# Zero products in TensorE's idle time, half-width contractions and a new order in a GQA decode and gated MLP backward kernel

## The chip, the cores and the metric

The kernel runs on one core of one Trainium2 chip. Times are device microseconds of one execution, from the runs' own clock. A profile is one execution recorded by the hardware; its span goes from the first to the last instruction of the program.

## The reference

A layer of one token for two sequences: grouped-query attention over a cache (32 query heads, 16 key heads, 4096 positions, head size 128) beside a gated MLP without activation (576 to 4608 and back), both on a layer-normed input, summed with the input. The kernel must give the output and the gradients of every input, all in bf16.

```
xn  = layernorm(x)                       # x: 2 x 1 x 576
q   = xn @ wq                            # 32 heads of 128
p   = softmax(q @ k_cache.T / sqrt(128)) # two query heads share one key head
a   = (p @ v_cache) @ wo
h   = (xn @ w_gate) * (xn @ w_up)
out = x + a + h @ w_down
# returned: out, and the vector-Jacobian product with grad_out for
# x, k_cache, v_cache, wq, wo, w_gate, w_up, w_down
```

The caches are 2 x 16 x 4096 x 128 each, and so are their gradients. The gradient of the values is an outer product of p and the output gradient, that of the keys an outer product of ds and q. So 92 MB are read, 92 MB are written, and little is computed on each element.

## The kernel before

**Work.** The attention goes in 16 steps: a step is one pair of key heads (a "group" of two) of one sequence, and loads four tiles of 1 MB, two of K and two of V, each 128 partitions by 4096. `load_kv` issues these loads on SyncE (SP); `load_ws` issues those of the weights, `put` the stores, on the same queue, in order. For each step:

- `turn` transposes K and V tiles in 32 x 32 blocks on VectorE (DVE), two instructions of 1024 fp32 pairs per tile, into another buffer of the pool `big`.
- `score` (L1205) multiplies the transposed tile by small stationaries `W`, 32 products a tile; four products with 32 output partitions stand side by side on the array.
- `softmax` and `dscore` turn the scores into p and ds through a chain of small products and copies on ScalarE (ACT), DVE and TensorE (PE) (L1267 to L1333), and `spread` brings them into the two layouts `pp` and `dd`.
- `contract` (L1378) multiplies the K or V tile as it was loaded by `pp` or `dd`: 16 products of 512 columns a step for each of K and V, in halves of 8, four side by side in one PSUM bank. Its end, with the transposes, sets the tile free for the next load (`free_kv`). The bank is copied to `osb` (L422 or L1388), and four products with `fold` (L1395) sum it into `oT`.
- `outer` and `head_outer` (L1226) make the outer products, two of 512 columns for each 128 x 1024 piece, into the three double banks `o`; ACT or DVE copies each piece to a 1 MB buffer of `big` (L422, L424), which `put` stores (L644).
- GpSimd builds the block-diagonal `BD` (L1193) and the stationaries `W` (L1170).

The MLP comes in nine pieces (`mlp`) with outer products of the same kind, and the gradients of wq and wo are made once a group (`group_back`).

**PSUM.** Six of the eight banks are the three double banks `o`; the two banks `m` serve all the rest, one user at a time.

**Order.** Nothing is scheduled at run time. While the program is built, the class `Order` plays through all streams of work with a cost for each operation, and writes each engine's instructions in the order in which they would start. Ties within a small slack go by the priorities `PRI`; `AT` says at which load of K or V the weights are loaded; `EV` lets each eviction go to ACT or DVE, whichever would be done first, with `BIAS` against DVE. A product's cost is its streaming time times `CLK`. The engines then run their lists in order and wait on semaphores, whatever the costs were.

```
def PE(stream, issue=0.0, quad=None, kind="f"):
    return ("op", "PE", max(CLK * stream, issue) + 0.03, quad, stream, issue, kind)
```

The functions that the change touches:

Of the kernel before, what the change touches and what calls it, by code (L numbers as in the profile page):

```python
# [63 lines left out]
class Order:  # L64
# [88 lines left out]
    def run(self):  # L153
        while self.streams:
# [94 lines left out]
def DMA(engine, cost, nbytes, row=8192):  # L249
# [7 lines left out]
    "turn0": [12127.5, 6592.3, 21769.7, -2605.1, 16027.7, 11327.0, 15999.3, 39550.4, 10382.6, -7734.4, 35538.2,  # L257
        24878.1, 2718.9, 31584.2, -26890.5, 2784.8],
    "turn1": [-17638.3, 2610.3, 11642.0, -23025.1, -666.2, 15183.7, -8429.9, 1153.7, -20487.3, 25941.4,
        10117.7, 4947.3, -2272.2, 26485.5, 30929.5, -2450.0],  # L260
    "W0": [17499.7, 23187.9, 23229.4, -24562.1, -25413.4, 21241.8, -52583.1, 25355.3, -4026.7, -26992.9,
        -2792.0, -39509.0, -20712.1, -23397.7, -38581.5, -1973.1],
    "W1": [-68220.0, -3785.6, -5692.6, -26672.7, -32830.2, -16110.0, -12761.0, -19860.2, 22087.6, 15126.8,
        -21980.3, 8805.5, -32643.6, 50340.4, -9766.7, -46949.6],
    "BD0": [33847.1, 15885.5, -3782.4, -11229.3, 24201.3, 31507.4, 16705.2, 36715.7, 22613.4, -26234.1,
        -2581.7, 109848.8, -44765.9, -8040.0, -3442.2, 23039.7],
    "BD1": [6023.1, 63457.9, 25871.9, 3200.3, 32198.5, -18814.1, 12365.4, 26532.9, 45847.1, -51895.6, 27362.3,
        -76393.3, 2863.2, -15443.1, -42340.1, -14044.7],
    "att": [-30329.0, -12134.6, -9680.1, 2262.2, -4349.2, 5413.2, -20317.8, -14023.7, -15815.4, -22206.1,
        -49797.4, -334.9, -19593.2, -20211.8, -68161.8, -27358.0],  # L270
    "dsc": [-23906.4, -34630.7, -2728.5, -23998.0, -19328.5, -8575.3, -10061.5, -15550.8, 13655.4, -23902.2,
        -28324.1, -40880.7, -28538.6, -56867.0, -5830.5, -12006.5],
    "conv": [-12341.8, -11809.0, -28772.8, 4652.6, -75297.7, -7012.1, -20664.5, 17461.5, 27449.8, 21658.4,
        -6850.8, -13921.3, -10206.6, -13431.8, 19855.6, -8570.5],
    "con": [-42900.2, 17788.3, 198.2, -17106.1, -21976.4, -3999.9, 7207.3, -22623.4, -6927.6, 21516.2, 20924.0,
        -13390.2, -118243.2, -7700.5, 19019.7, 14780.5],
    "out0": [22678.2, 12788.2, 42398.2, 31027.3, 49279.4, -11087.6, 5917.5, 42793.0, -20399.7, 57105.8,
        29375.6, 687.4, 24906.2, -2550.4, -27276.1, 33869.5],
    "out1": [19262.8, 2604.4, 2928.7, 23228.2, 21627.8, -10501.4, 15188.8, 7961.4, 18967.4, 20607.5, 11898.0,
        33332.1, 33685.2, 22220.0, 30731.2, 4846.1],  # L280
    "load": [27975.6, -31596.9, -27237.7, 3512.0, -22563.4, -17007.1, 4137.9, 25122.5, 5758.3, -9052.6,
        -35105.2, 2003.7, -28928.7, 6812.9, 23298.4, -60102.7],
    "front": [22268.9, 9016.8, -3195.4, -925.0, -11488.9, -5594.5, -10266.7, 2816.4],
    "back": [8334.8, 3131.5, 10704.4, -20159.0, -16008.9, -4698.0, -5371.8, 1371.3],
    "mlp": [-5535.1, -15193.4, -221.7, -14784.7, -3773.2, 8812.5, 807.2, 180.8, 6936.3],
    "mload": [-52363.2, -31069.0, 25120.7, -76464.9, 11215.5],
    "wload": [26545.8, -25483.3, -28807.4, 17849.2, -51701.7, -14210.9, -857.7, -9350.9, -12979.9, -24368.0,
        -173571.7, -10429.5, -11015.2, 13337.1, -10805.0, 6634.5],
    "wout": [-3917.3],
    "store": [6257.1],  # L290
    "fin": [-45349.8],
    "const": [46567.9],
}
AT = {
    "wq": [-5, 7, 11, 24, 31, -18, 50, -5],
    "wo": [-13, -2, -15, 2, 36, -14, 47, 53],
    "mlp": [2, 16, -13, 39, 111],
# [13 lines left out]
def kernel(  # L311
# [81 lines left out]
    osb_t = tiles("osb", 1, [P, 4, P])  # L393
# [15 lines left out]
    m_t = banks("m", 2, [P, 512])  # L409
# [29 lines left out]

    eps_t = filled("eps_t", [2, 1], FP32, EPS)  # L440
# [38 lines left out]
    fold = const.tile([P, 4, GH], BF16, name="fold")  # L479
    foldf = ch_t[0]["ex"][:, 80:80 + 4 * GH].rearrange("p (w r) -> p w r", w=4)  # L480
# [6 lines left out]
    def consts():  # L487
# [18 lines left out]
        for w in range(4):  # L506
            sums(foldf[:, w].rearrange("p (l r) -> p l r", l=2), [[32, 2], [1, 2], [64, 2]], 4 * w)
# [746 lines left out]
    def softmax(s):  # L1254
# [6 lines left out]
        for l in range(G):  # L1261
            yield PE(0.427, 0.224, kind="c")
            score(0, s, sc, l)
            yield REL("X", xS[s][0][l])
        yield REL("W0", wS[s][0])
# [15 lines left out]
        nc.tensor.matmul(mT[:, 256:257], lhsT=c["mr"][:], rhs=one1[:], start=True, stop=True)  # L1281
        yield DVE(0.14)
        nc.vector.tensor_scalar(c["negb"][:], mT[:, 256:257], -SCALE, None, op0=ALU.mult)  # L1283
# [26 lines left out]
    def dscore(s):  # L1310
# [4 lines left out]
        for l in range(G):  # L1315
            yield PE(0.427, 0.224, kind="c")
            score(1, s, dp, l)
            yield REL("X", xS[s][1][l])
        yield REL("W1", wS[s][1])
# [41 lines left out]
    def contract(s, t):  # L1361
# [11 lines left out]
        for part in range(2):  # L1373
            yield PE(0.427, 0.056, kind="c")
            for k in range(8 * part, 8 * part + 8, 4):
                for j in range(4):
                    c, l = k + NCH // 2 * (j // 2), j % 2
                    nc.tensor.matmul(ct[32 * j:32 * j + 32, :], lhsT=view(rT, 0, P, 4 * c + 2 * l, [[1, 32]]),  # L1378
                                     rhs=kv_t[kvS[s][t][l]][:, Dh * c:Dh * (c + 4)],
                                     start=(k == 0), stop=(k == NCH // 2 - 4))  # L1380
# [3 lines left out]
        e = yield EV(512)  # L1384
# [8 lines left out]
        yield PE(0.0, 0.104)  # L1393
        for w in range(4):
            nc.tensor.matmul(m_t[m][:, 0:GH], lhsT=osb_t[i][:, w], rhs=fold[:, w], start=(w == 0), stop=(w == 3))  # L1395
# [138 lines left out]
```

## Time and profile before

| | |
|---|---|
| median of 3 runs | 472.77 us (471.36 to 472.91) |
| the profiled execution | 471.37 us |
| its span | 469.6 us |
| mean granted TensorE clock in it | 0.71 |
| HBM read, written | 92.48 MB, 92.48 MB |

A row of a group gives line, engine, operation, output and inputs, shape, count, then busy us, mean ns of one, and the idle time in front of them with what ended it. PEld is the weight load, which runs beside the products. A window's row gives start:end, length, busy us (and instructions) of PE, PEld, DVE, ACT and POOL, then the granted clock, the mean busy share of the 16 DMA engines, and GB/s. In the 40 slices of the page each digit is a tenth of the slice's time.

### The profile page before, as it was taken

The page shows a single profiled execution, that of the slowest core. Times are in us where ns is not written, and L with a number is a line of the kernel's source. Part 1 is how long each engine was busy: PE and PEld are TensorE (multiplying, and loading weights), DVE is VectorE, ACT ScalarE, POOL GpSimd, SP SyncE. Part 2 cuts the span into 40 slices and gives each one's busy share as a digit, 9 for nine tenths or more (in the row PEclk, how much of TensorE's full clock was granted, in tenths as well). Part 3 has the DMA queues.
Part 4 walks back from the last instruction along what each step waited for, and adds up shares of the span by engine and source line. Part 5 has one row for each costly group of instructions (what it writes and reads, how often), then busy time and mean ns, then how long its engine had stood idle before and what let it go on. Part 6 is the DMA issues. An engine that isn't in the chain of part 4 may idle for free.

```text
span 469.6 us, 15459 instructions
## 1 busy us (share of the span) xinstructions
PE 370.8 (79%) x6636; PEld 217.5 (46%) x6636; DVE 369.5 (79%) x705; ACT 334.3 (71%) x507; POOL 146.8 (31%) x176
## 2 busy tenths in 40 slices
PE   0588688869887777986997669789699898998984
PEld 0455444435653352554463444564345434444453
DVE  9689878967867879688689658978867978898772
ACT  2149668867885948671798638877678678789973
POOL 3350242681330320203252264000843705325100
PEclk9978897767757668776675767956656658566977
DMA  8999999999999999999999999999999989999995
GB/s 317 404 413 403 363 390 419 409 416 421 418 416 420 399 421 406 412 415 419 399 418 404 386 418 424 408 413 342 413 416 393 424 270 416 423 413 413 424 368 176
DMA packets 40053, 185.96 MB, mean 396 GB/s; under 512 B 3496, under 2 KB 11184, under 8 KB 23600
## 3 DMA queue, kind: packets, MB, share of 16 engines
q1 hardware_dynamic: 39976, 184.96, 98.1%
q8 instruction: 52, 0.85, 0.7%
q14 instruction: 17, 0.14, 0.1%
q10 hardware_dynamic: 8, 0.00, 0.0%
HBM read 92.48 MB, written 92.48 MB: 394 GB/s over the span
## 4 chain that ended last, share of the span: by engine, by line
PE 42%; ACT 18%; DVE 18%; DMA 12%; issue 5%; POOL 2%; SPq 2%; ACTq 0%; DVEq 0%; POOLq 0%
ACT big L422 15%; DMA out_dram<-big 10%; DVE big L418 8%; PE ps_m L1378 8%; PE ps_o L1226 7%; PE ps_m L1205 7%; PE ps_o L675 4%; PE ps_m L841 3%; DVE big L424 3%; DMA big<-in_A_v_cache_dram 3%; PE ps_m L967 2%; PE ps_m L636 2%; POOL BD L1193 2%; PE ps_o L712 1%; SPq L1129 1%
## 5 line engine op out<-in xcount | busy, mean ns | idle before, releaser
L422 ACT CAST big<-ps_o 128x1024 bf16<-128x1024 f32 (+4 forms) x319 | 279.7, 950 | 40.3 <-PE ps_o L1226 18.2
L418 DVE STREAM_TRANSPOSE big<-big 128x1024 f32<-128x1024 f32 x146 | 176.1, 1223 | 5.9 <-DMA big<-in_A_v_cache_dram 3.6
L1193 POOL TENSOR_TENSOR BD<-vr,mask 128x2048 bf16<-128x2048 bf16 x32 | 115.2, 3603 | 198.8 <-ACT vr L422 122.2
L424 DVE CAST big<-ps_o 128x1024 bf16<-128x1024 f32 (+2 forms) x71 | 78.2, 1102 | 15.8 <-PE ps_o L675 5.2
L1205 PE MATMUL ps_m<-big,W 128*32 128x128 bf16 x2048 | 57.1, 274 | 5.5 <-ACT osb L422 0.7
L1226 PE MATMUL ps_o<-BD,dd 32*128 32x512 bf16 x256 | 48.8, 489 | 12.7 <-ACT big L422 9.2
L1205 PEld LDWEIGHTS <-W 128*32 128x32 bf16 x2048 | 45.4, 121 | 21.9 <-issue 18.6
L1226 PE MATMUL ps_o<-BD,pp 32*128 32x512 bf16 x256 | 42.1, 461 | 10.4 <-ACT big L422 6.7
L1170 POOL COPY W<-rep 32x16 bf16<-32x16 bf16 x128 | 24.5, 192 | 63.5 <-DVE rep L951 53.2
L418 DVE STREAM_TRANSPOSE big<-ww 128x1152 f32<-128x1152 f32 (+1 forms) x25 | 32.9, 1317 | 4.5 <-DMA out_dram<-big 3.3
L1378 PE MATMUL ps_m<-big,pp 128*32 128x512 bf16 x256 | 28.2, 536 | 1.5 <-DVE small L1330 1.2
L1378 PE MATMUL ps_m<-big,dd 128*32 128x512 bf16 x256 | 27.5, 518 | 1.5 <-DVE dd L418 0.6
L1226 PEld LDWEIGHTS <-dd 32*128 32x128 bf16 x256 | 11.8, 97 | 32.4 <-issue 24.7
L1226 PEld LDWEIGHTS <-pp 32*128 32x128 bf16 x256 | 10.4, 95 | 26.9 <-issue 22.6
L422 ACT CAST osb<-ps_m 128x512 bf16<-128x512 f32 x15 | 8.9, 590 | 15.9 <-PE ps_m L1378 12.6
L675 PE MATMUL ps_o<-dyr,R 32*32 32x288 bf16 x256 | 17.3, 402 | 2.0 <-ACT big L422 2.0
L675 PE MATMUL ps_o<-dyr,hb 32*32 32x288 bf16 x288 | 16.5, 346 | 1.1 <-ACT big L422 0.9
L967 PE MATMUL ps_m<-big,Wdy 128*128 128x128 bf16 x144 | 14.9, 285 | 3.1 <-DVE small L1283 2.0
L712 PEld LDWEIGHTS <-xnr 32*128 32x128 bf16 x368 | 12.5, 119 | 9.3 <-issue 8.6
L422 ACT CAST sp<-ps_m 128x256 bf16<-128x256 f32 x22 | 8.4, 380 | 11.2 <-PE ps_m L1213 11.0
L636 PEld LDWEIGHTS <-wm 128*32 128x32 bf16 x704 | 13.4, 115 | 6.3 <-issue 5.1
L841 PE MATMUL ps_m<-big,Wdy 128*128 128x128 bf16 x162 | 15.6, 272 | 0.6 <-DVE small L1291 0.4
(210 smaller groups left out, 481.9 us busy)
## 6 DMA issues: line engine op xcount, KB each, us to landing
out_dram<-big SPq DMA_DIRECT2D x74, 1024.0 KB, 12.1
big<-in_A_k_cache_dram SPq DMA_DIRECT2D x32, 1024.0 KB, 12.4
big<-in_A_v_cache_dram SPq DMA_DIRECT2D x32, 1024.0 KB, 12.5
out_dram<-big SPq DMA_DIRECT2D x17, 576.0 KB, 11.4
ww<-in_B_w_down_dram SPq DMA_DIRECT2D x9, 576.0 KB, 11.1
ww<-in_A_wo_dram SPq DMA_DIRECT2D x8, 576.0 KB, 11.1
ww<-in_A_wq_dram SPq DMA_DIRECT2D x8, 512.0 KB, 11.6
big<-in_B_w_gate_dram SPq DMA_DIRECT2D x4, 1024.0 KB, 13.1
```

The lines of the kernel that those rows point to most:

```text
L418: nc.vector.transpose(out, in_)
L422: nc.scalar.copy(out, in_)
L424: nc.vector.tensor_copy(out=out, in_=in_)
L636: nc.tensor.matmul(dp[32 * q:32 * q + 32, :], lhsT=view(Wm[:], 0, P, 8 * pos(q, s), [[1, 32]]), rhs=view(X, 0, P, xoff(q, s), [[FS, blocks ...
L675: nc.tensor.matmul(o[32 * q:32 * q + 32, aa, 0:HD2], lhsT=view(t, 32 * q, 32, 2 * A + aa, [[4, 32]]), rhs=dyr[32 * q:32 * q + 32, k * HD2: ...
L841: nc.tensor.matmul(dh, lhsT=Wdy[:, e, 2 * k:2 * k + P], rhs=view(X[:], 0, P, 64 * k + e, [[D, FC], [2, 32]]), start=(k == 0 and e == 0), s ...
L967: nc.tensor.matmul(dp, lhsT=Wdy[:, e, 2 * k:2 * k + P], rhs=view(X[:], 0, P, 64 * k + e, [[D, GH], [2, 32]]), start=(k == 0 and e == 0), s ...
L1170: nc.gpsimd.tensor_copy(view(W_t[t][w][:], 32 * a, 32, 6 + 8 * a, [[G * WW, 4], [WW, G], [1, 2]]), view(rep_t[grp[g]["qs"]][:], 32 * a, 32 ...
L1193: nc.gpsimd.tensor_tensor(BD_t[i][:], view(vr_t[v][:], 0, P, 0, [[0, 16], [1, Dh]]), view(mask16[:], 0, P, 0, [[1, 16], [0, Dh]]), ALU.mult)
L1205: nc.tensor.matmul(sc[32 * cq:32 * cq + 32, :], lhsT=view(W[:], 0, P, (be * G + l) * WW + 6 - 4 * c2 - 2 * l, [[1, 32]]), rhs=view(X[:], 0 ...
L1226: nc.tensor.matmul(o[:, k, :], lhsT=pr2[32 * c4:32 * c4 + 32, :], rhs=BD[32 * c4:32 * c4 + 32, 8 * l + 4 * h2:8 * l + 4 * h2 + 4, :], star ...
L1378: nc.tensor.matmul(ct[32 * j:32 * j + 32, :], lhsT=view(rT, 0, P, 4 * c + 2 * l, [[1, 32]]), rhs=kv_t[kvS[s][t][l]][:, Dh * c:Dh * (c + 4) ...
```

## The change

Three things are changed.

Whenever the planner puts an operation on PE later than PE would be free, it now writes zero products ahead of it: 70% of the planned gap, in products of 256 columns counted at 0.1079 us times CLK, at most 40. They multiply the identity by a stationary of zeros (128 x 32) and write 32 partitions of columns 256 to 511 of a bank `m`: the first of the two that no open accumulation holds (`held`).

For this, all users of `m` keep to columns 0 to 255. The contraction makes products of 256 columns instead of 512, twice as many, into half a bank; `osb` is half as wide, and `fold` sums two pieces instead of four.

All priorities, the places of the weight loads, CLK (1.65 to 1.5), BIAS and the slacks are new, and with them the order of the instructions on every engine and of the DMAs on SP.

```diff
+        self.idle, self.fill = 0, lambda n: None
...
                 if e == "PE":
+                    gap = t - self.free[e] - FILL[0]
+                    self.idle = min(40, int(FILL[1] * gap / (FILL[2] * CLK))) if gap > 0 else 0
+                    self.fill(self.idle)
...
-CLK = 1.65
-BIAS = 0.21111771427708687
-SLACK = {"PE": 0.0, "ACT": 0.11786185086953341, "DVE": 0.44815392421950667, "POOL": 1e9, "SP": 1e9}
+CLK = 1.5
+FILL = (0.1, 0.7, 0.1079)
+BIAS = 0.14496977787064985
+SLACK = {"PE": 0.0, "ACT": 0.12111524253408697, "DVE": 0.4771875031870091, "POOL": 1e9, "SP": 1e9}
...
-    m_t = banks("m", 2, [P, 512])
+    m_b = banks("m", 2, [P, 512])
+    m_t = [t[:, 0:256] for t in m_b]
...
+    none = filled("none", [P, 32], BF16, 0.0)
+    held = set()
+
+    def keep(n):
+        b = min(set(range(2)) - held, default=None)
+        for _ in range(n if b is not None else 0):
+            nc.tensor.matmul(m_b[b][0:32, 256:512], lhsT=none[:], rhs=view(ident[:], 0, P, 0, [[0, 2], [1, P]]),
+                             start=True, stop=True)
+
+    od.fill = keep
...
         for part in range(2):
-            yield PE(0.427, 0.056, kind="c")
-            for k in range(8 * part, 8 * part + 8, 4):
+            yield PE(0.427, 0.42, kind="c")
+            held.add(m)
+            for k in range(8 * part, 8 * part + 8, 2):
                 for j in range(4):
                     c, l = k + NCH // 2 * (j // 2), j % 2
                     nc.tensor.matmul(ct[32 * j:32 * j + 32, :], lhsT=view(rT, 0, P, 4 * c + 2 * l, [[1, 32]]),
-                                     rhs=kv_t[kvS[s][t][l]][:, Dh * c:Dh * (c + 4)],
-                                     start=(k == 0), stop=(k == NCH // 2 - 4))
+                                     rhs=kv_t[kvS[s][t][l]][:, Dh * c:Dh * (c + 2)],
+                                     start=(k == 0), stop=(k == NCH // 2 - 2))
+        held.discard(m)
...
-        e = yield EV(512)
+        e = yield EV(256)
...
-        for w in range(4):
-            nc.tensor.matmul(m_t[m][:, 0:GH], lhsT=osb_t[i][:, w], rhs=fold[:, w], start=(w == 0), stop=(w == 3))
+        for w in range(2):
+            nc.tensor.matmul(m_t[m][:, 0:GH], lhsT=osb_t[i][:, w], rhs=fold[:, w], start=(w == 0), stop=(w == 1))
```

More of the change, by code (lines that the diff above doesn't have):

```diff
@@ L256 @@
 PRI = {
[L257 to L292, printed above, removed]
+    "turn0": [25647.0, 30933.0, 59651.5, 8573.8, 24596.6, 25586.7, 16157.6, 66777.4, 8012.9, -11937.5, 67193.2,
+        21446.2, 58693.9, 71054.9, -66770.6, -12337.9],
+    "turn1": [-58372.6, 2200.4, -25266.6, 38458.6, -369.3, 43908.9, -65242.7, -95764.2, 4720.8, 29312.5, 159.2,
+        11362.9, 25680.8, 66371.2, -7700.9, 3779.4],
+    "W0": [4231.0, 91170.0, 98227.9, -44267.9, 90751.9, 114299.8, 11718.5, 38256.0, -36166.4, -101497.1,
+        20204.6, -146953.5, -8683.6, -30617.3, -31627.8, -10413.7],
@@ new lines @@
+    "load": [132316.4, -5590.6, 10219.3, -54870.8, -28969.6, 89662.0, 75493.6, -71120.2, 51498.1, -62326.4,
+        -53925.5, -66113.9, -19595.9, 16922.9, 89410.0, 50484.2],
+    "front": [13723.8, 46497.3, -24176.4, 8763.4, -63700.8, 16607.5, 383.5, 24119.0],
+    "back": [-16156.9, 18212.3, 46475.2, -99761.2, -53662.6, 28098.5, 3400.5, -73405.5],
+    "mlp": [-16968.8, -12624.8, 6427.1, 6716.6, -5850.8, 23248.6, 16011.1, 5180.2, 34400.5],
+    "mload": [-145581.1, 2457.1, 64254.3, -109850.0, -12241.8],
@@ L293 @@
+    "wload": [10120.4, -83088.5, -16095.3, 27183.6, -45170.7, -32644.0, 40938.0, -51817.6, -40539.8, 6993.9,
+        -151246.4, -31748.4, -111127.8, -41554.8, 34957.3, 46055.8],
+    "wout": [-8532.8],
+    "store": [72290.7],
+    "fin": [-60767.3],
+    "const": [55048.0],
 }
 AT = {
-    "wq": [-5, 7, 11, 24, 31, -18, 50, -5],
-    "wo": [-13, -2, -15, 2, 36, -14, 47, 53],
-    "mlp": [2, 16, -13, 39, 111],
+    "wq": [0, 8, -15, 9, 33, 37, 7, 48],
+    "wo": [-18, -20, -19, 22, 35, 0, 43, 2],
@@ L298 @@
+    "mlp": [6, -14, -9, 44, 61],
 }
@@ L392 @@
     dd_t = tiles("dd", 2, [P, 2, P])
-    osb_t = tiles("osb", 1, [P, 4, P])
+    osb_t = tiles("osb", 1, [P, 2, P])
     od.ring("ch", 2)
@@ L478 @@
     mask16 = const.tile([P, 16], BF16, name="mask16")
-    fold = const.tile([P, 4, GH], BF16, name="fold")
-    foldf = ch_t[0]["ex"][:, 80:80 + 4 * GH].rearrange("p (w r) -> p w r", w=4)
+    fold = const.tile([P, 2, GH], BF16, name="fold")
+    foldf = ch_t[0]["ex"][:, 80:80 + 2 * GH].rearrange("p (w r) -> p w r", w=2)
     Exn, Exr, Edy, Econst, Ezero = Event(), Event(), Event(), Event(), Event()
@@ L1262, in softmax @@
             yield PE(0.427, 0.224, kind="c")
+            held.add(k)
             score(0, s, sc, l)
             yield REL("X", xS[s][0][l])
+        held.discard(k)
         yield REL("W0", wS[s][0])
@@ L1316, in dscore @@
             yield PE(0.427, 0.224, kind="c")
+            held.add(k)
             score(1, s, dp, l)
             yield REL("X", xS[s][1][l])
+        held.discard(k)
         yield REL("W1", wS[s][1])
@@ L1392, in contract @@
         m = yield ACQ("m")
-        yield PE(0.0, 0.104)
-        for w in range(4):
-            nc.tensor.matmul(m_t[m][:, 0:GH], lhsT=osb_t[i][:, w], rhs=fold[:, w], start=(w == 0), stop=(w == 3))
+        yield PE(0.0, 0.052)
+        for w in range(2):
+            nc.tensor.matmul(m_t[m][:, 0:GH], lhsT=osb_t[i][:, w], rhs=fold[:, w], start=(w == 0), stop=(w == 1))
         yield REL("osb", i)
```

22 lines of the change are left out of this document (20 added, 2 removed).

## The prediction

> **What bounds the kernel now.** I read first the page's busy times and slices, then windows cut where the DMA row dips, then what the load queue (SyncE, SP) waits for in the dips, then the groups that the change touches.
>
> ```profile
> span 469.6 us, 15459 instructions
> PE 370.8 (79%) x6636; PEld 217.5 (46%) x6636; DVE 369.5 (79%) x705; ACT 334.3 (71%) x507; POOL 146.8 (31%) x176
> PEclk9978897767757668776675767956656658566977
> DMA  8999999999999999999999999999999989999995
> q1 hardware_dynamic: 39976, 184.96, 98.1%
> ```
>
> No compute engine is full, while the sixteen DMA engines carry packets for 98.1% of the span. The windows give, behind the time, the busy us of PE, PEld, DVE, ACT and POOL, then granted clock, DMA share and GB/s:
>
> ```profile
> 0.00:14.00 14.00, 1.76 (x14) 0.85 (x15) 12.78 (x61) 4.54 (x7) 4.26 (x8) 1.00 0.87 329
> 14.00:440.00 426.00, 348.38 (x6205) 203.45 (x6204) 338.37 (x606) 310.49 (x473) 142.52 (x168) 0.70 1.01 405
> 375.00:380.00 5.00, 4.75 (x60) 2.19 (x58) 4.41 (x8) 3.50 (x5) 0.02 (x1) 0.50 0.59 204
> 440.00:455.00 15.00, 13.38 (x238) 8.10 (x240) 13.43 (x23) 12.91 (x18) 0.00 (x0) 0.83 1.01 420
> 455.00:465.00 10.00, 7.29 (x190) 5.13 (x190) 4.92 (x19) 6.40 (x10) 0.00 (x0) 0.84 0.70 247
> 465.00:469.60 4.60, 0.00 (x0) 0.00 (x0) 0.00 (x0) 0.00 (x0) 0.00 (x0) 0.50 0.12 41
> ```
>
> From 14 to 440 us the share is 1.01, so the DMAs set the pace there and a quicker engine buys nothing, except in one hole at 375 to 380, and then at the end. The hole costs 5 x (1.01 - 0.59) = 2.1 us, the stretch 455 to 465 costs 10 x (1.01 - 0.70) = 3.1 us. The last 4.6 us are the final landing and stay. In the hole PE is busy 4.75 of 5 us at half clock. What the queue did around it:
>
> ```profile
> 360.31 10.28 SPq L644 DMA_DIRECT2D out_dram<-big  x5
> 378.41 0.34 SPq L1087 DMA_DIRECT2D big<-in_A_v_cache_dram  x1
> SPq L1087 <- PE ps_m L1378: 7.8, 1, 7.8
> 376.00 1.05 PE ps_m L1378 x8
> 377.37 0.97 PE ps_m L1378 x8
> ```
>
> After five stores the next load stood 7.8 us until the contraction (L1378) had given back its V buffer at 378.4. What was in flight drained meanwhile. So the kernel is bound by DMA, with about 5 us lost where PE is late.
>
> **The change part by part.** The DMAs are the same set in both programs: 220 on SP, of the same shapes. What can change is only when they are issued.
>
> *Contraction in 256 columns.*
>
> ```profile
> L1378 PE MATMUL ps_m<-big,pp 128*32 128x512 bf16 x256 | 28.2, 536 | 1.5 <-DVE small L1330 1.2 <-ACT sp L422 0.3
> L1378 PE MATMUL ps_m<-big,dd 128*32 128x512 bf16 x256 | 27.5, 518 | 1.5 <-DVE dd L418 0.6 <-DVE small L1283 0.5 <-DVE wm L629 0.2
> 442.20 0.62 PE L1378 MATMUL ps_m<-big,dd 128*32 128x512 bf16 x8
> L1205 PE MATMUL ps_m<-big,W 128*32 128x128 bf16 x2048 | 57.1, 274 | 5.5 <-ACT osb L422 0.7 <-issue 0.7 <-POOL W L1170 0.7
> ```
>
> 512 products become 1024 of half the width, so the columns streamed, and the 28.2 + 27.5 = 55.7 us, stay. Each has its own weight load, so 512 loads are added. The scores (L1205) issue a load with every 128-column product at 57.1 / 2048 = 28 ns a pair; 16 pairs of a half contraction would take 0.45 us, under the 0.62 us that it takes at full clock and the 0.97 us at half clock. They hide under the streaming: 0. Were that cover gone, the bound is 64 halves x 0.45 = 29 us of PE, nearly all in PE's idle time. Below zero there is the fold: 128 products become 64, a few us of PE off the path.
>
> *Evictions.*
>
> ```profile
> L422 ACT CAST big<-ps_o 128x1024 bf16<-128x1024 f32 x249 | 238.8, 1032 | 27.7 <-PE ps_o L1226 18.2 <-DMA out_dram<-big 4.2 <-PE ps_o L712 3.4
> L424 DVE CAST big<-ps_o 128x1024 bf16<-128x1024 f32 x57 | 68.9, 1208 | 8.3 <-PE ps_o L1226 4.4 <-PE ps_o L712 2.6 <-issue 0.7
> L422 ACT CAST big<-ps_o 128x576 bf16<-128x576 f32 x59 | 35.6, 651 | 10.9 <-PE ps_o L675 8.8 <-DMA out_dram<-big 1.6 <-ACT big L422 0.2
> L424 DVE CAST big<-ps_o 128x576 bf16<-128x576 f32 x9 | 6.7, 749 | 5.3 <-PE ps_o L675 5.2
> L422 ACT CAST osb<-ps_m 128x512 bf16<-128x512 f32 x15 | 8.9, 590 | 15.9 <-PE ps_m L1378 12.6 <-DVE small L1322 3.3
> L422 ACT CAST sp<-ps_m 128x256 bf16<-128x256 f32 x22 | 8.4, 380 | 11.2 <-PE ps_m L1213 11.0
> ```
>
> The osb copies halve: 590 ns against 380 for the same shape as sp, so 0.2 us on each of 32. That sits behind the release of the K or V buffer, so it moves no load. The new order shifts work too. By the two instruction lists the 1024-column evictions go from 249 on ACT and 57 on DVE to 235 and 71, the 576-column ones from 59 and 9 to 53 and 15. DVE gains 14 x 1.21 + 6 x 0.75 = 21 us and reaches about 391 us (83%); ACT, with 14 x 1.03 + 6 x 0.65 + 8.5 us less, falls to about 307. Neither is full, 0 on the path; but DVE now has the least room.
>
> *Zero products.* The changed list holds 392 of 32 x 256: 50 around the first two products, where PE is busy 1.76 of 14 us, and 342 in 144 small groups later, mostly one to three. Their price comes from the contraction, where eight 512-column products pass four side by side, in two rounds: 0.97 us at half clock, 0.62 at full. So 256 columns take 0.62 / 4 = 0.16 to 0.97 / 4 = 0.24 us, and 342 take 53 to 83 us. PE's idle time from 14 to 465 us is 451 - 348.4 - 13.4 (its busy time from 440 to 455) - 7.3 = 82 us. At full clock they fit, at half clock they fill it. I take a value between, most of them at half clock, about 70 us: no cost at the DMA-bound places, up to all of it where PE is late.
>
> What do they buy? Granted clock does not follow PE's busy time alone:
>
> ```profile
> 290.00:300.00 10.00, 9.20 (x227) 5.87 (x225) 9.45 (x19) 9.29 (x15) 0.27 (x1) 1.00 1.01 411
> 400.00:410.00 10.00, 9.76 (x155) 4.97 (x147) 7.95 (x15) 7.54 (x13) 2.79 (x1) 0.50 1.01 425
> PE ps_m L1328 <- DVE small L1322: 5.8, 4, 2.5
> ```
>
> PE was as busy from 400 to 410 as from 290 to 300, at half the clock. Columns streamed would tell these apart better; counted from both lists, zero products add 100 thousand to 1.19 million, 8%. So I expect the mean clock to go from 0.71 to about 0.74, not to 1. Idle gaps are short already: 2.5 us (L1328) is the longest wait of a product from 20 to 465 us. The Trainium skill (TensorE: Matmul & The Clock Gate, Why this matters for your kernels) says that idle gaps over about 3 us drop the clock; by that rule it would hardly fall here at all, and the row at 0.50 disagrees.
>
> The products are not free of waits: of the first of each group, 99 carry one, 75 on DVE and 23 on ACT, for the last reader of that bank. The PE queue is in order, so the next score, contraction or outer product stands behind it, and the eviction and the store behind that. The wait's bounds are zero, where the next product waits as long anyway, and an osb-sized read of 0.6 us; I take 0.1 us, 10 us of PE in all, hidden while PE has room. The Trainium skill (PSUM — Partial Sum Buffer, PSUM bank collisions raise a hardware error) says that two engines on one bank and quadrant collide even in different columns; that fits these waits, and no run here shows a collision.
>
> *New order.* By the SP lists the longest run of stores ahead of a load falls from 10 to 7, so a load stands behind fewer late stores, as the one at 378 did. Behind the last load there are 16.7 MB to store against 12.5: inputs end earlier by some 10 us of transfer, and the last MLP piece, whose work stands in the final stretch, comes ahead of the last V loads. Against it, two stores of 1 MB are now nearly last where 64 KB pieces were. These I weigh together: I take the hole (2.1 us) as gone and half of the end's 3.1 us, 1.5, less 0.4 us for zero products in the way of the last evictions: 3.2 us.
>
> **The sum.** The profiled execution took 471.37 us, 1.77 us beyond its span and 1.4 us under the median of 472.77. 471.37 - 3.2 = 468.2; with the 1.4 us back, 469.6.
>
> **The rivals.** *PE runs cold and full (slower).* The search counts on faster products (CLK 1.5 for 1.65) and on short zero products. If the clock stays near 0.71, PE carries 370.8 + 70 + 10 = 451 us of 470, 96%, and contractions free K and V buffers late. The place is SP's load behind the contraction, as at 378; one such hole costs 2.1 us. It decides once PE has under some 5% of idle left from 14 to 440 us. Two holes more than now give 472.8 + 4.2 = 477.0. For it: 9.76 us busy at 0.50. Against it: the DMAs hold the pace at 1.01 with PE at 82%.
>
> *The gate counts idle time (faster still).*
>
> ```profile
> 50.00:55.00 5.00, 2.38 (x44) 1.36 (x40) 4.71 (x11) 4.24 (x8) 0.00 (x0) 0.90 0.97 310
> 250.00:255.00 5.00, 4.29 (x19) 1.64 (x18) 4.87 (x6) 5.00 (x9) 0.00 (x0) 0.50 0.97 407
> 255.00:260.00 5.00, 3.41 (x83) 2.34 (x83) 4.70 (x8) 2.52 (x4) 3.71 (x5) 0.62 0.94 379
> 315.00:320.00 5.00, 3.95 (x59) 1.54 (x56) 1.76 (x5) 2.09 (x4) 0.00 (x0) 0.50 0.96 386
> 325.00:330.00 5.00, 4.43 (x62) 1.46 (x63) 4.67 (x7) 3.18 (x6) 0.27 (x1) 0.50 0.90 319
> 385.00:390.00 5.00, 3.66 (x36) 2.60 (x34) 4.32 (x8) 4.84 (x9) 1.53 (x8) 0.84 0.97 365
> ```
>
> The zero products close the gaps and the clock goes to 0.85 or more; real PE work then shrinks by more than the zero products take. The hole, all of the end's 3.1 us and these shallow dips (1.01 less each share, times 5 us: 1.8 us) go: 472.8 - 7.0 = 465.8. Against it: the busy stretch at 0.50 from 400 to 410. The gap rule of the Trainium skill named above would ask for this.
>
> *Nothing moves.* The order mends one hole and makes another; 472.8. For it: DMA share 1.01 over 426 us.
>
> **How the numbers follow.** Forecast 469.6 with chance 0.38 (its own range 467 to 471.3), clock rival 0.14, no change 0.13, cold PE 0.35. This kernel's measurement tells 0.3%, 1.4 us, from no change. Faster 0.52, same 0.13, slower 0.35. The range takes in the clock rival, down to 464.5, and the cold rival with its two holes and some more, up to 478.5.
>
> **What would show it.** Right: clock between 0.72 and 0.77, PE busy about 430 us, no window from 15 to 440 us with a DMA share under 0.9, and 455 to the end shorter. Wrong: a load waiting over 5 us on L1399 (the contraction after the change) with a DMA share near 0.6 (cold PE); a clock over 0.85 (the gate counts idle); DVE in over 0.95 of the stretches before such holes would put DVE in PE's place.

## The result and the profile after

The changed kernel takes 493.23 us (median of 4 runs, 490.74 to 496.13), the kernel before 472.06 us on the same chip (470.53 to 472.91): a ratio of 1.045, 95% interval 1.038 to 1.053. It is 21 us slower, and above the range of the prediction (464.5 to 478.5). The profiled execution took 496.13 us, the longest of the four; its clock was 0.769 in the mean. Of the runs below, one of four each in the kernels with medians of 479.9 and 485.1 us was slow (485.4 and 487.4 us) and is left out of the ratio.

The page of the changed kernel, the lines that answer to those shown of before:

```profile
span 494.4 us, 17154 instructions
PE 413.5 (84%) x7476; PEld 260.1 (53%) x7476; DVE 392.7 (79%) x735; ACT 310.0 (63%) x476; POOL 147.1 (30%) x176
PEclk9557889877795789687667757898877598676877
DMA  8998999998999999988999994999999989999795
q1 hardware_dynamic: 39976, 184.96, 94.4%
PE 47%; DVE 25%; ACT 11%; DMA 8%; issue 7%; SPq 0%; DVEq 0%; ACTq 0%
DVE big L424 12%; PE ps_m L452 9%; ACT big L428 8%; PE ps_m L1399 7%; PE ps_o L1242 6%; PE ps_m L1221 6%; DVE big L430 5%; DMA big<-in_A_k_cache_dram 5%; PE ps_o L691 4%; PE ps_o L728 2%; PE ps_m L857 2%; PE ps_m L983 2%; DMA gu<-in_B_w_up_dram 1%; PE ps_m L652 1%; DMA out_dram<-big 1%
```

The same bytes went the same way, and the packets took about as long: 94.4% of 494.4 is 467 us, 98.1% of 469.6 was 461. But the DMA engines stood still for 494.4 - 467 = 28 us instead of 9. That is 19 of the 25 us between the spans. The last two lines are the chain that ended last: the zero products (L452), which no result needs, are 9% of it, some 44 us. They were meant to lie in idle time; on this chain, others wait for them.

The windows say where the DMAs stood still (columns as in the prediction; the last three are granted clock, DMA share, GB/s):

```profile
14.00:440.00 426.00, 360.05 (x6640) 228.02 (x6640) 340.23 (x601) 268.25 (x416) 138.22 (x167) 0.76 0.97 384
45.00:50.00 5.00, 4.76 (x73) 2.42 (x62) 3.93 (x9) 3.92 (x8) 3.61 (x1) 0.77 0.41 123
120.00:125.00 5.00, 5.00 (x144) 3.21 (x138) 3.94 (x8) 4.49 (x6) 0.00 (x0) 0.76 0.71 247
220.00:225.00 5.00, 4.13 (x84) 2.21 (x84) 4.89 (x11) 4.99 (x7) 0.00 (x0) 1.00 0.62 215
295.00:300.00 5.00, 3.29 (x18) 2.15 (x17) 4.01 (x6) 0.00 (x0) 0.78 (x4) 0.50 0.50 206
300.00:305.00 5.00, 4.82 (x125) 3.57 (x123) 2.04 (x5) 0.92 (x3) 3.96 (x4) 0.67 0.22 48
395.00:400.00 5.00, 4.58 (x109) 2.90 (x102) 4.75 (x12) 3.38 (x5) 0.00 (x0) 0.96 0.64 223
460.00:465.00 5.00, 4.05 (x73) 2.53 (x66) 4.25 (x8) 3.46 (x5) 0.00 (x0) 0.97 0.50 205
```

Where the kernel before had one hole ahead of its end, there are six up to 465 us (295 to 305 is one). The longest is 295 to 305. What SP waited for ahead of the K load of 302.80 us (total, times, longest), and the two DMAs that it issued around the wait:

```profile
SPq L1103 <- DVE small L1350: 8.7, 1, 8.7
SPq L1103 <- PE ps_m L1399: 4.9, 1, 4.9
```

```profile
288.77 0.42 SPq L1128 DMA_DIRECT2D ww<-in_A_wo_dram  x1
302.80 0.33 SPq L1103 DMA_DIRECT2D big<-in_A_k_cache_dram  x1
```

For 13.6 us (8.7 + 4.9) SP issued nothing: the next K load needs a buffer that the contraction L1399 gives back, and that stands behind the softmax chain. This is PE in that chain (start, us, line; in brackets the idle time ahead and its releaser):

```profile
285.42 0.37 PE L1293 MATMUL ps_m<-identf,small 128*1 128x128 f32 x1
286.22 1.22 PE L452 MATMUL ps_m<-ident,none 128*32 128x256 bf16 x5 [0.43 <-DVE small L1295]
287.37 0.58 PE L1299 MATMUL ps_m<-one,sp 1*128 1x1 f32 x2
288.20 0.37 PE L452 MATMUL ps_m<-ident,none 128*32 128x256 bf16 x1 [0.25 <-DVE small L1301]
...
297.95 2.29 PE L452 MATMUL ps_m<-ident,none 128*32 128x256 bf16 x10 [1.43 <-DVE small L1350]
300.18 0.29 PE L1201 MATMUL ps_m<-ident,qr 128*128 128x128 bf16 x1
...
300.86 1.90 PE L1399 MATMUL ps_m<-big,pp 128*32 128x256 bf16 x32 [0.18 <-ACT vr L428]
```

Read the row of 297.95. The planner saw PE idle until DVE (L1350) was done, and wrote ten zero products into that gap. But they go to a bank `m` that the same DVE instruction has yet to read, and DVE does two transposes first. PE idles 1.43 us, the reader ends, and only then the ten products start: 2.29 us, ahead of the link (L1201) that could have started. They lie behind the gap and not in it. The chain that ended last in this stretch, in order of time (start, us, line), shows them between the reader and the link:

```profile
295.50 2.36 DVE big L424 x2
297.86 0.06 DVE small L1350
297.95 2.29 PE ps_m L452 x10
300.24 0.23 PE ps_m L1201
```

So it is with all eight groups between the first link and the contraction (three are shown): PE waits ahead of each. The stretch ran at half clock throughout:

```profile
284.00:301.00 17.00, 12.44 (x75) 7.56 (x71) 6.56 (x14) 2.46 (x8) 1.99 (x10) 0.50 0.80 334
```

### The profile page after: what moved, and what is told of

Its sections match the earlier page's. It is cut to its first block, busy times and chain, and to the rows that moved or that the text cites. A ratio compares the mean times of both kernels' runs of the same rounds, so it can differ in the third digit from the quotient of the medians.

```text
span 494.4 us, 17154 instructions
## 1 busy us (share of the span) xinstructions
PE 413.5 (84%) x7476; PEld 260.1 (53%) x7476; DVE 392.7 (79%) x735; ACT 310.0 (63%) x476; POOL 147.1 (30%) x176
## 3 DMA queue, kind: packets, MB, share of 16 engines
q1 hardware_dynamic: 39976, 184.96, 94.4%
## 4 chain that ended last, share of the span: by engine, by line
PE 47%; DVE 25%; ACT 11%; DMA 8%; issue 7%; SPq 0%; DVEq 0%; ACTq 0%
DVE big L424 12%; PE ps_m L452 9%; ACT big L428 8%; PE ps_m L1399 7%; PE ps_o L1242 6%; PE ps_m L1221 6%; DVE big L430 5%; DMA big<-in_A_k_cache_dram 5%; PE ps_o L691 4%; PE ps_o L728 2%; PE ps_m L857 2%; PE ps_m L983 2%; DMA gu<-in_B_w_up_dram 1%; PE ps_m L652 1%; DMA out_dram<-big 1%
## 5 line engine op out<-in xcount | busy, mean ns | idle before, releaser
L428 ACT CAST big<-ps_o 128x1024 bf16<-128x1024 f32 (+3 forms) x300 | 263.3, 942 | 51.3 <-PE ps_o L1242 27.8
L452 PE MATMUL ps_m<-ident,none 128*32 128x256 bf16 x392 | 87.6, 341 | 50.7 <-DVE small L1350 6.0
L430 DVE CAST big<-ps_o 128x1024 bf16<-128x1024 f32 (+3 forms) x90 | 100.2, 1114 | 15.9 <-PE ps_o L691 7.1
L452 PEld LDWEIGHTS <-none 128*32 128x32 bf16 x392 | 41.0, 111 | 64.6 <-issue 53.1
L1242 PE MATMUL ps_o<-BD,dd 32*128 32x512 bf16 x256 | 41.7, 418 | 4.5 <-ACT big L428 2.5
L1242 PE MATMUL ps_o<-BD,pp 32*128 32x512 bf16 x256 | 40.4, 440 | 3.3 <-ACT big L428 2.4
L1399 PE MATMUL ps_m<-big,pp 128*32 128x256 bf16 x512 | 29.0, 363 | 1.0 <-ACT vr L428 0.9
L1399 PE MATMUL ps_m<-big,dd 128*32 128x256 bf16 x512 | 27.8, 353 | 0.4 <-DVE dd L424 0.2
L1242 PEld LDWEIGHTS <-dd 32*128 32x128 bf16 x256 | 10.8, 93 | 21.0 <-issue 16.4
L1399 PEld LDWEIGHTS <-pp 128*32 128x32 bf16 x512 | 17.4, 121 | 8.4 <-issue 5.1
L1242 PEld LDWEIGHTS <-pp 32*128 32x128 bf16 x256 | 10.1, 96 | 18.3 <-issue 15.3
L1399 PEld LDWEIGHTS <-dd 128*32 128x32 bf16 x512 | 14.6, 116 | 8.2 <-issue 4.5
L428 ACT CAST vr<-ps_m 128x128 bf16<-128x128 f32 x21 | 5.7, 271 | 20.5 <-PE ps_m L1201 20.4
```

Of the source, the lines that this page charges most:

```text
L428: nc.scalar.copy(out, in_)
L430: nc.vector.tensor_copy(out=out, in_=in_)
L452: nc.tensor.matmul(m_b[b][0:32, 256:512], lhsT=none[:], rhs=view(ident[:], 0, P, 0, [[0, 2], [1, P]]), start=True, stop=True)
L1242: nc.tensor.matmul(o[:, k, :], lhsT=pr2[32 * c4:32 * c4 + 32, :], rhs=BD[32 * c4:32 * c4 + 32, 8 * l + 4 * h2:8 * l + 4 * h2 + 4, :], star ...
```

## The experiments

The two causes that the diff offers are the order and the zero products. For the zero products there are three readings: PE's time in them, the wait in PE's queue, or the place that the wait gives them. Within each half of the table, all instructions but the zero products stand in the same sequence on all five engines. Ratios are to the kernel before, run on the same chip, with 95% intervals; the medians of before were 471.3 to 472.5 us. The clock is that of the profiled execution.

| zero products | count, with a wait | us | ratio | clock |
|---|---|---|---|---|
| *new order* | | | | |
| the change | 392, 99 | 493.2 | 1.045 (1.038–1.053) | 0.769 |
| none | 0 | 480.3 | 1.018 (1.016–1.021) | 0.698 |
| one a group, 2 columns | 146, 99 | 485.1 | 1.022 (1.015–1.030) | 0.687 |
| one a group | 146, 99 | 489.2 | 1.038 (1.032–1.045) | 0.704 |
| fewer (share 0.48) | 250, 90 | 485.3 | 1.030 (1.024–1.035) | 0.735 |
| in free banks, share 0.7 | 249, 17 | 473.0 | 1.003 (1.000–1.005) | 0.748 |
| in free banks, share 1.0 | 373, 20 | 473.5 | 1.001 (0.998–1.003) | 0.807 |
| in free banks, share 1.5 | 582, 25 | 473.4 | 1.005 (1.003–1.007) | 0.830 |
| *order of before, 256 columns* | | | | |
| none | 0 | 473.4 | 1.003 (1.000–1.006) | 0.712 |
| one a group, 2 columns | 127, 82 | 477.1 | 1.011 (1.007–1.015) | 0.692 |
| as in the change | 293, 82 | 480.9 | 1.020 (1.017–1.022) | 0.774 |
| in free banks, share 0.7 | 181, 21 | 471.7 | 1.000 (0.997–1.003) | 0.724 |
| in free banks, share 1.0 | 280, 23 | 473.9 | 1.005 (1.003–1.007) | 0.734 |

**Taking the change apart.** The change without its zero products:

```diff
-        for _ in range(n if b is not None else 0):
+        for _ in range(0):
```

> The changed kernel with every zero product left out; the order of all other instructions and of the DMAs is that of the changed kernel. If the zero products make it slow (their own 88 us on TensorE and their waits in its queue), this comes back to 468 to 475 us, PE busy near 365 us, granted clock back to about 0.71 and no DMA window of 10 us under a share of 0.9 between 20 and 450 us. If the new order itself is at fault, because it counts on products at CLK 1.5 that the chip does not give, this stays at 488 us or goes above 494, as the lower clock then makes TensorE later still. If it is half and half: 480 to 485 us.

480.3 us: the new order with half-width contractions alone loses 8, and the zero products the other 13. This split holds for parts taken off in this sequence; the runs in free banks below show that the two do not simply add. The same chain without them, in the timeline and the windows of this kernel:

```profile
277.33 0.37 PE L1293 MATMUL ps_m<-identf,small 128*1 128x128 f32 x1 [0.40 <-DVE small L1285]
278.97 0.58 PE L1299 MATMUL ps_m<-one,sp 1*128 1x1 f32 x2 [1.27 <-ACT sp L1297]
...
287.51 0.27 PE L1201 MATMUL ps_m<-ident,qr 128*128 128x128 bf16 x1 [1.73 <-DVE small L1350]
...
288.20 0.62 PE L1399 MATMUL ps_m<-big,pp 128*32 128x256 bf16 x8
```

```profile
276.00:288.50 12.50, 6.91 (x79) 5.06 (x74) 6.28 (x15) 2.47 (x8) 2.15 (x10) 0.50 1.01 419
```

At the same half clock it takes 288.20 - 277.33 = 10.9 us to the contraction, against 300.86 - 285.42 = 15.4 in the change, and the DMA share stays at 1.01. Over the whole run, the loads of K and V (L1103) wait less without zero products behind outer products (L1242: 14.9 us in all, against 22.1 in the change) and behind L1350 (3.6 against 8.7), but not behind contractions (L1399: 27.4 against 24.4). So the hole above is one case; what the loads wait for differs from hole to hole.

The zero products in the order of before (the numbers of the search and the two planner costs of the contraction put back):

```diff
-CLK = 1.5
+CLK = 1.65
...
-            yield PE(0.427, 0.42, kind="c")
+            yield PE(0.427, 0.056, kind="c")
```

> The order of the kernel before (its priorities, CLK 1.65 and its costs in the planner, so SP's list is the same), with contractions of 256 columns and with zero products in its planned gaps: 293 of them instead of 392. If zero products make the time: by their count 472 + 21 x 293/392 = about 488 us, with new DMA holes. If the order makes it: 470 to 474 us, and a clock above 0.71 at no loss.

480.9: they cost some 8 us there too, by 1.020 against 1.003 without them (the run below). So it isn't peculiar to one order.

The kernel before with the half-width contraction alone (the same edit, without zero products):

> The kernel before with contractions of 256 columns alone: its own order, no zero products. The forecast's price of this part is 0 us: 470 to 474 us. A theory in which the 512 added weight loads and the narrower products hold up TensorE gives its bound, up to 29 us of TensorE, and some 478 to 490 us.

473.4, by its interval between nothing and 3 us. The reverse, the new order with products of 512 columns and no zero products (the kernel before with the new numbers of the search):

```diff
-CLK = 1.65
-BIAS = 0.21111771427708687
+CLK = 1.5
+BIAS = 0.14496977787064985
...
-            yield PE(0.427, 0.056, kind="c")
+            yield PE(0.427, 0.42, kind="c")
```

> The order of the changed kernel alone: contractions of 512 columns as before, no zero products, the planner's costs as in the changed kernel so that SP's list is the same. If the order is at fault: 488 us or more, as the run without zero products. If zero products are at fault: 468 to 475 us. Against that run it also shows the price of the narrower contraction under this order: 0 to 2 us by the forecast.

479.9 us, ratio 1.015 (1.010 to 1.020), as the new order with 256 columns. So the width costs 3 us at the most, and the 8 us without zero products are the order's.

**The bank.** The zero products go only into a bank, of `o` or `m`, that the plan has free since before the gap; where there is none, none are written:

```diff
-        b = min(set(range(2)) - held, default=None)
-        for _ in range(n if b is not None else 0):
-            nc.tensor.matmul(m_b[b][0:32, 256:512], lhsT=none[:], ...
+        at = od.free["PE"]
+        free = [t[0:32, c] for tag, ts, c in (("o", [t[:, 0] for t in o_t], slice(0, 256)), ("m", m_b, slice(256, 512)))
+                for i, t in enumerate(ts) if od.slots[tag][i] is not None and when(od.slots[tag][i]) <= at]
+        for _ in range(n if free else 0):
+            nc.tensor.matmul(free[0], lhsT=none[:], ...
```

> The changed kernel with its order, but a zero product is written only into a bank (of m or of o) that the plan shows free, read to the end before the gap begins: 249 products, of which 68 stand behind a reader that they wait for, 32 of these at the start, instead of 392 with 281 behind one. Against 480.3 us without zero products and 493.2 with all: if the loss is the products that wait for a reader and then run when the gap is over, 480 to 483 us, or a little under 480 if the clock helps. If it is TensorE's time for zero products wherever they stand, 480.3 + 12.9 x 249/392 = 488.5 us.

473.0: not only is the loss of the zero products gone, the new order is 7 us faster with them than without. Counted from the two instruction lists, of the 99 gaps with a wait in the change 52 still hold products here, 13 of them behind a wait, and 47 hold none. So the run does not tell a better bank from leaving such a gap empty. As many products at the banks of the change, by a smaller share of the gap:

```diff
-FILL = (0.1, 0.7, 0.1079)
+FILL = (0.1, 0.48, 0.1079)
```

> The changed kernel with 48% of each planned gap filled instead of 70%: 250 zero products, as many as in the run with free banks, but placed as in the changed kernel, 185 of them in 90 groups behind a reader. If standing behind a reader is what costs: about 489 us, well above the run with free banks. If only the number of products counts: 488.5 us, the same as that run. If the waits as such cost, whatever stands behind them: 480.3 + 12.9 x 90/99 = 492 us.

485.3 with 250 products against 473.0 with 249: where they may stand decides, not the count. One product a group instead of all:

```diff
-        for _ in range(n if b is not None else 0):
+        for _ in range(min(n, 1) if b is not None else 0):
```

> The changed kernel with one zero product in each group: the same 146 places and 99 waits, but 146 products instead of 392, 99 behind a reader. If the waits as such hold TensorE's queue: 492 to 493 us, as with all. If it is the time of the products behind them: about 480.3 + 12.9 x 98/249 = 485 us.

489.2 us. With 146 of the 392 products, 9 of the 13 us are there. That is more than with 250 products; the clock (0.704 against 0.735) is one reason that could be, and no run separates it. The order of before with zero products in free banks (both edits above):

> The order of the kernel before, contractions of 256 columns, and zero products in free banks only: 181 products, 71 behind a reader (32 of these at the start). Against 473.4 us without zero products in this order and 480.9 with 293, 198 behind a reader. If standing behind a reader is what costs: 472 to 475 us, and if the raised clock is then a gain, a little under 472. If all time on zero products costs: 473.4 + 7.5 x 181/293 = 478 us.

471.7, no different from the kernel before.

**The wait or the time.** As the run with one product a group, but 2 columns wide, so that the wait stays and next to nothing is streamed:

```diff
-            nc.tensor.matmul(m_b[b][0:32, 256:512], lhsT=none[:], rhs=view(ident[:], 0, P, 0, [[0, 2], [1, P]]),
+            nc.tensor.matmul(m_b[b][0:32, 256:258], lhsT=none[:], rhs=ident[:, 0:2],
```

> The changed order with one zero product per group and only 2 columns wide instead of 256, so the groups' waits for the readers of their banks stay and the streamed zero columns are all but gone. Theory A, it is the wait in PE's in-order queue that costs: as with one full product per group, 487 to 490 us. Theory B, it is PE's time in the zero columns: 480 to 482, as with no zero products at all. Half of each: 484 to 486.

485.1 in the median, but its runs lie from 479.4 to 487.4, and its interval takes in the run without zero products: between the two theories, and inconclusive by itself. The order of before was steadier:

> The order of before, contraction in 256 columns, and in every group of zero products just one, 2 columns wide: the groups' 82 waits for readers stay, the columns are gone. Theory A, the waits cost: most of what 293 full products cost there, 477 to 481. Theory B, the products' time behind the waits costs: 472 to 475, as this order without any zero product (473.4).

477.1 us. Of what 293 full products cost there, 1.020 - 1.003, the waits alone give 1.011 - 1.003: about half, and by the intervals anything from a fifth to four fifths. So the waits cost something by themselves, with the pass of even the smallest product; that the rest is the time of the products behind them is likely but not shown, as the clock differed too (0.692 against 0.774).

Nearly as many products as in the change, in free banks:

```diff
-FILL = (0.1, 0.7, 0.1079)
+FILL = (0.1, 1.0, 0.1079)
```

> The changed order with nearly as many zero products of full size as the change has (373 against 392), but only in banks that are planned free since before the gap (20 of the groups still carry a wait, 99 in the change). Theory A, the readers' waits cost: near the free-bank run with 249 products, 472 to 476. Theory B, TensorE's time in the products costs: 485 to 493, as the change itself.

473.5, a ratio of 1.001. This run and the change differ in the banks, in the spread (80 groups against 146) and in 19 products, and in 20 us. Its page and windows:

```profile
span 468.7 us, 17116 instructions
PE 395.6 (84%) x7457; PEld 254.0 (54%) x7457; DVE 391.2 (83%) x735; ACT 308.6 (66%) x476; POOL 147.1 (31%) x176
q1 hardware_dynamic: 39976, 184.96, 98.2%
```

```profile
14.00:440.00 426.00, 363.59 (x7058) 234.00 (x7054) 360.87 (x640) 287.57 (x448) 142.81 (x168) 0.81 1.01 405
```

PE is as busy between 14 and 440 us as in the change (363.59 and 360.05 us), and the DMA share is back at 1.01. The same chain:

```profile
262.60 0.37 PE L1295 MATMUL ps_m<-identf,small 128*1 128x128 f32 x1
262.90 1.67 PE L454 MATMUL ps_o<-ident,none 128*32 128x256 bf16 x8
264.50 0.38 PE L1301 MATMUL ps_m<-one,sp 1*128 1x1 f32 x2
...
269.60 1.81 PE L454 MATMUL ps_o<-ident,none 128*32 128x256 bf16 x15
272.51 0.22 PE L1203 MATMUL ps_m<-ident,qr 128*128 128x128 bf16 x1 [1.10 <-DVE small L1352]
...
273.13 1.06 PE L1401 MATMUL ps_m<-big,pp 128*32 128x256 bf16 x32
```

Here fifteen products run at once, while DVE works, and PE still waits 1.10 us for DVE before L1203 (the L1201 of the change, two lines on). From the first link to the contraction, 37 zero products take 6.0 us of PE's time by the timeline, and 23 took 6.2 us in the change. The chain takes 273.13 - 262.60 = 10.5 us with the ones and 15.4 with the others. Part of that can be the warmer clock (0.87 in this stretch by the windows); at half clock and without zero products it was 10.9. The groups of the two kernels:

```profile
L452 PE MATMUL ps_m<-ident,none 128*32 128x256 bf16 x392 | 87.6, 341 | 50.7 <-DVE small L1350 6.0 <-ACT sp L428 3.6 <-ACT vr L428 3.1
```

```profile
L454 PE MATMUL ps_o<-ident,none 128*32 128x256 bf16 x343 | 59.6, 316 | 1.4 <-POOL ident masks.py:199 1.4
L454 PE MATMUL ps_m<-ident,none 128*32 128x256 bf16 x30 | 6.3, 307 | 0.0
```

In the change PE stood idle for 50.7 us ahead of zero products, behind readers; in free banks for 1.4. What the loads wait for changes with it (total, times, longest; the first row is the change, the others are the run in free banks, its lines two on):

```profile
SPq L1103 <- DMA out_dram<-big: 4.8, 4, 2.4
SPq L1105 <- DMA out_dram<-big: 26.3, 13, 9.9
SPq L1105 <- PE ps_m L1401: 10.4, 4, 4.7
```

Behind contractions they stand 10.4 us instead of 24.4, and the largest sum is now for stores to land. Last, more of them than fit:

```diff
-FILL = (0.1, 1.0, 0.1079)
+FILL = (0.1, 1.5, 0.1079)
```

> The changed order and zero products only in banks that are planned free, but 582 of them instead of 373 (fill share 1.5, so each group is half as long again as its planned gap; the change has 392). Theory A, only waits for readers cost while PE has room, and a warmer clock pays for the products: 472 to 476. Theory B, PE's time in zero products that overrun their gap costs too: 478 to 490.

473.4. Even 582 products, half as long again as their planned gaps, leave the kernel within 0.5% (0.3 to 0.7) of the kernel before. PE's time in zero products isn't what was short. In the order of before, a share of 1.0 in free banks:

> The order of before, contraction in 256 columns, zero products only into banks that are planned free since before the gap, and more of them (fill share 1.0 instead of 0.7: 280 instead of 181). Theory A, products that wait for nobody cost nothing and raise the clock: at or under 471.7, down to 470. Theory B, PE's time itself is short: 473 to 476. The kernel before is 472.

473.9: no gain, and 0.5% (0.3 to 0.7) slower than the kernel before. None of these versions beats the kernel before by what can be measured.

**The order's 8 us.** The first theory was the planner's assumed speed: the new order counts on faster products (CLK 1.5), which the chip gives only when zero products warm it. Each order with the other's assumption, without zero products:

```diff
-CLK = 1.65
+CLK = 1.5
```

> The kernel before with one number of the search changed: the planner counts on products that are as fast as the new order counts on (CLK 1.5 instead of 1.65). No zero products, 512 columns. Theory A, the new order loses because it is planned on a PE that the chip doesn't give: 476 to 482, as the new order alone. Theory B, it is the order's priorities and not the assumed PE speed, or the order of before is good by selection and not by its assumption: A would be told from this by the reverse run. If the planned speed does not matter: 472 to 475.

```diff
-CLK = 1.5
+CLK = 1.65
```

> The reverse: the new order's priorities and no zero products, planned with CLK 1.65 instead of 1.5. Theory A, the assumed speed of PE is at fault: 473 to 476 (new order without zero products 480.3). Theory B, the priorities and choices are at fault, or any replanning scatters so far: 479 to 483.

498.3 us, ratio 1.056 (1.054 to 1.059), and 494.4 us, ratio 1.049 (1.044 to 1.053). Both swaps lose, in both directions, more than the new order did. By the theory the second should have been mended. But both orders were planned anew, and that alone may cost as much. The kernel before, planned anew with its assumption changed by under 1%:

```diff
-CLK = 1.65
+CLK = 1.64
```

> The kernel before, replanned with the assumed speed of the products changed by under 1% (CLK 1.64 for 1.65). The two lists of PE are alike to about the 147th small tile and then differ. If any replanned order scatters by as much as the new order loses: 477 to 490. If close parameters give close times: 471 to 474, and the new order's 8 us would be its own.

485.8 us, ratio 1.027 (1.022 to 1.033). One of its windows:

```profile
385.00:390.00 5.00, 4.39 (x108) 3.31 (x100) 4.75 (x9) 2.75 (x5) 3.11 (x1) 0.82 0.33 109
```

So a step of under 1% in one number costs more than the new order's 8 us. The hole here has another cause than the one above: its load stood 11.9 us until a store had landed, and not behind a contraction. An order is good as one particular list, and so the two swaps cannot decide about the theory. The runs in free banks speak for it: the same new list, at a clock of 0.748 to 0.830, is within 0.5% of the kernel before, and 1.8% slower at 0.698. No run raises the clock of this list without zero products, so that the warmer clock is what mends it stays open.

## Why the prediction was wrong, point by point

**What bounds the kernel.** Right as a description; wrong as the shield that the prediction made of it. That the DMAs set the pace and a quicker engine buys nothing held from 473 us on: in free banks the clock went from 0.748 to 0.81 and 0.83, and the time stayed. But the prediction turned it round: a later PE was to cost nothing while PE has idle time. The loads go to buffers that PE's chain gives back, and what has slack is each chain, not PE's sum. The windows with a share under 0.9 that were to be absent are there.

**Contraction.** Right, as near as the run tells (0 to 3 us). The two groups stream 29.0 + 27.8 = 56.8 us against 55.7:

```profile
L1399 PE MATMUL ps_m<-big,pp 128*32 128x256 bf16 x512 | 29.0, 363 | 1.0 <-ACT vr L428 0.9
L1399 PE MATMUL ps_m<-big,dd 128*32 128x256 bf16 x512 | 27.8, 353 | 0.4 <-DVE dd L424 0.2
```

**Evictions.** DVE was put at 391 us and ACT at 307; they are at 392.7 and 310.0, neither full. Right.

**Time of the zero products.** 87.6 us for 392 is 0.22 us each, inside 0.16 to 0.24, and PE's 413.5 us are under the 430 expected; the clock came out at the top of its range. The size was right; "no cost at the DMA-bound places" was not, for the reason of the next step.

**The waits: the step that failed.** The prediction found them: 99 first products with a wait for the last reader of their bank. It priced the wait (0.1 us each) and hid it in PE's idle time. It did not ask where the product lies once the wait is over: ahead of the next link, with its whole group behind it. By the rows above a group of one then adds 0.37 us to its chain at half clock, a group of ten 2.29. In all that was 13 us against the run without zero products, where the sum had 0.4 us, for the last evictions alone. With 20 waits for 99 and nearly the whole count of products, nothing was lost that could be measured. The wait comes from sharing a bank; the Trainium skill (PSUM — Partial Sum Buffer, PSUM bank collisions raise a hardware error) says that accesses of two engines to one bank and quadrant collide even in different columns. No run here leaves such a wait out, so whether the chip needs it isn't shown; that it costs is.

**The new order: the other step that failed.** Put at 3.2 us of gain, it lost 8 without zero products and came out even, 0 to 2 us slower, with them in free banks; the gain showed in no run. The sum credited it with the known hole and charged it with none of its own, and the runs of replanned orders show how unsafe that is: they lost 13 to 27 us on the same work. The end was no gain either. In the change the last load is issued at 436.7 us of 494.4, and before at 426.3 of 469.6, so that 57.7 us stand behind it instead of 43.3. With 373 products in free banks it is issued at 413.4 of 468.7: the inputs do end earlier, as forecast, and the end is longer by nearly as much, 55.3 us. Nothing in the profile of before could price the holes of an order that had not run; the bounds of this step should have been tens of us on the slow side.

**The clock.** 0.74 was forecast, "0.72 to 0.77", and 0.769 came. That it goes with columns streamed is borne out below.

**The rivals.** Cold PE had the direction right, and the place in part (loads behind the contraction, but behind the outer products as well), but neither the condition nor the price: PE was 85% busy from 14 to 440 us (360.05 of 426) and warmer than before, and the run in free banks was as busy without loss. Where it counted two holes more, there are five more. The sign that was set for it came: ahead of 215.15 us a load waited 5.1 us on L1399, and the DMA share was 0.86 from 215 to 220 us and 0.62 from 220 to 225. The K load issued at 222.71 had waited 7.0 us for an outer product, though. In the whole run (total, times, longest):

```profile
SPq L1103 <- PE ps_m L1399: 24.4, 8, 5.1
SPq L1103 <- PE ps_o L1242: 22.1, 9, 7.0
```

It is a sign of late contractions, whatever makes them late; the kernel before had such a wait too, of 7.8 us. The sign for DVE did not come: in the 5 us ahead of each of these holes DVE was busy 4.52 us at the most. The clock rival's condition, 0.85 or more, did not come, and at 0.83 the time was 473.4 us, not 465.8. That nothing moves was refuted by the result.

## What to carry to other kernels

Filler for an idle engine has to be ready before the gap begins: if it shares a bank with whoever makes the engine wait, it starts when the gap ends, and stands in front of the work that the gap was waiting for. (A shared tile or buffer should do the same; only the bank was run.) So look in the list of a changed kernel for what each filler waits for, and price not the wait but everything that then stands ahead of the next link. And where an order has been searched, treat any replanned order as a new draw: measure it without the other edits before crediting it with anything. Its cost need not add to theirs: here it was 8 us without filler and nearly nothing with filler in free banks.

## What the runs showed of the hardware

In these runs TensorE's clock went with the columns streamed. Products of 2 columns, one in each group, left it at 0.687, against 0.698 without any; in the order of before it was 0.692 against 0.712. In free banks 249 products of 256 columns gave 0.748, 373 gave 0.807 and 582 gave 0.830, though the stationary was 32 columns of zeros. What counts is columns in a time, not in all: the change has more products (392) than the run with 373 but takes longer, streams 2612 columns a us of its span against 2745 (1.292 million in 494.4 us, 1.287 million in 468.7), and its clock is 0.769 against 0.807. PE's busy share does not tell: it is 81% in the 2-column run and 79% without zero products, where the clock is higher. That is an agreement over runs; what the throttle measures isn't shown. The windows of the 2-column run and of the 582, with PE busy 83% and 87% of the time:

```profile
14.00:440.00 426.00, 353.61 (x6636) 226.55 (x6638) 348.08 (x616) 276.54 (x429) 138.93 (x167) 0.68 0.99 395
```

```profile
14.00:440.00 426.00, 370.66 (x7155) 241.32 (x7155) 357.62 (x631) 284.79 (x443) 142.53 (x168) 0.83 1.00 400
```

The Trainium skill (TensorE: Matmul & The Clock Gate, Why this matters for your kernels) names idle gaps of over about 3 us as what drops the clock. In the kernel before, no wait of a product from 20 to 465 us was longer than 2.5 us, and the clock was 0.71 all the same, so gaps of that length do not account for it here.
